# Four groups' softmax weights turned on TensorE instead of through DRAM, and one weight tile split earlier, in a fused attention and MLP kernel

## The chip, the cores and the metric

The kernel runs on one core of a Trainium2 chip. The metric is device time in microseconds (us) of one execution. Engines: PE is TensorE (matmuls; PEld loads its weights), DVE is VectorE, ACT is ScalarE, POOL is GpSimd, SP is SyncE, which here issues nearly all transfers. SPq and the like are an engine's sequencer.

## The reference

Three stages in float32, each feeding the next:

```python
# attention inside chunks of 64 rows; B=4, H=8, S=576, D=64
scores = scale * np.matmul(q_c, k_c.transpose(0, 1, 2, 4, 3))
scores = scores - np.max(scores, axis=-1, keepdims=True)
attn = np.exp(scores)
attn = attn / (np.sum(attn, axis=-1, keepdims=True) + 1e-09)
out = np.matmul(attn, v_c)
x = out.transpose(0, 2, 1, 3).reshape(B * S, H * D)        # 2304 x 512
# first MLP: 512 -> 2048 -> 512
h = x @ w_in
g = np.maximum(h, 0.0) + alpha * np.minimum(h, 0.0)
x = g @ w_out
# second MLP: 512 -> 1536 twice, their product, -> 512
a = x @ w_a
b = x @ w_b
return a * b @ w_out
```

## The kernel before

**Tiles.** Tokens are worked in five blocks of 512, 256, 512, 512 and 512 (b = 0 to 4), and attention in 18 groups u of 128 tokens, two chunks of each of the eight heads at a time. Every float32 operand of an MLP matmul is split into a rounded high part and the remainder (names ending in h and l; `to_hi` on ACT, `to_lo` on DVE), and each product is made of three matmuls, high by high, low by high, high by low. The last two blocks are worked as a pair, with sums and differences of blocks and of weights (names p, t, ys, wit; the banks psA, psB, psD, psE), so that seven products do the work of eight.

**Loops.** The first three blocks run through 16 slices j of the hidden dimension each: twelve matmuls into psh (line 392), the bend on ACT and DVE (neg, pos, gh, gl), twelve matmuls into acc. The attention of the pair, groups 10 to 17, is woven into the loop of block b = 2, from about 174 to 300 us, by `att_line` (line 1065): a table gives each step its slot, and slot 2j or 2j + 1 stands beside slice j. The order on every engine is the order in which the code emits; nothing reorders it.

**One group's way.** POOL loads k and q of a group (`load_kq`, line 245) into a staging tile. `apart` has ACT split each into two planes of 16-bit halves (kqd, line 262) and SP write these to rows in DRAM (rowsk, rowsq, line 264). `turn_qk` has SP read them back transposed (kT, qT; DMA_TRANSPOSE, line 269). `multiply` makes the scores (`att_S`, line 311, bank psSO) and in the same two banks, with the transposed weights of a group three places earlier, the output (`att_O`, line 368). `soften` takes the maximum, exp (line 332), the sum and the division; the result is e, the softmax weights. The output's matmuls need e transposed (eT). For groups from `P_DMA` = 10 on, `att_PT_out` splits e on ACT (ed, line 262) and has SP write rowse; `att_PT_in`, two slots later, has SP read it back transposed as eT. For groups 0 to 9, `att_PT` does the same on chip: four transposes on PE (line 350) into a bank psP, and one ACT copy (line 352). psP comes from a pool of four banks that psh and psSO use as well.

SP's queue is in order: an instruction that waits for rows to land holds all behind it.

**The pair's first MLP.** `group1(jp)` (line 1366 and on) works two slices of the pair's weights at once. While one group of products runs, the steps of the next group's weights (`t_steps`: the sums and differences wit, and the splits Txh and Txl, txh and txl) are collected in a list, and `rest()` emits them at the end of the group's other work.

Of the kernel before, what the change touches and what calls it, by code (L numbers as in the profile page):

```python
# [18 lines left out]
def chunk_attention_prelu_mlp_bilinear_mlp(  # L19
# [19 lines left out]
    B, H, S, D = q.shape  # L39
# [6 lines left out]
    KD = DM // P  # L46
# [42 lines left out]
    def to_lo(hi, lo, src):  # L89
        if lo is None:  # L90
            return
        nc.vector.tensor_tensor(out=lo, in0=src, in1=hi.bitcast(F32), op=ALU.subtract)  # L92
# [164 lines left out]
    P_DMA = 10  # L257
# [82 lines left out]
        yield nc.vector.reciprocal(out=rc, in_=sm)  # L340
        yield nc.vector.tensor_tensor(out=e3, in0=e3, in1=rc.to_broadcast([P, H, CH]), op=ALU.mult)

    def att_PT(u):
        e_ = att.pop(("e", u))
        if u >= P_DMA:
            att["eT", u] = turned(halves(e_, wtile(f"ed{u}", F32), f"e{u}"), f"eT{u}")
            return
        ps = att_bank(u, "psP")
        for g in range(KD):
            nc.tensor.transpose(ps[:, g * P:(g + 1) * P], e_[:, g * P:(g + 1) * P], ident)  # L350
        t = wtile(f"eT{u}", F32)
        nc.scalar.activation(out=t, in_=ps, func=AF.Copy)
        att["eT", u] = t
# [185 lines left out]
    def stagger(chains):  # L539
        steps = [c[0] for c in chains[:1]]  # L540
        for i, c in enumerate(chains):
            steps += [d[0] for d in chains[i + 1:i + 2]] + c[1:]
        return steps
# [521 lines left out]
    def att_line(bx, x, ut, sums_of):  # L1065

        t0, n = blocks[bx]
        us = range(t0 // P, NU)
        LAG = 3

        def dest(u):
            if u * P < t0 + n:
                return *x, u * P - t0
            ut[u] = wtile(f"x{u}", F32).rearrange("p (k t) -> p k t", k=KD)
            return ut[u], None, 0

        def out_of(u, pss):
            o = att_O(u, *dest(u), pss)
            if u + LAG < NU:
                load_v(u + LAG, nc.gpsimd)  # L1080
            return o

        def multiply(w):
            pss = [bank("psSO") for _ in range(2)]
            now, then_ = us[w:w + 1], us[max(w - LAG, 0):max(w - LAG + 1, 0)]
            for u in now:
                att_S(u, [ps[:, :KD * CH] for ps in pss])
            o = sum((out_of(u, [ps[:, KD * CH:] for ps in pss]) for u in then_), [])
            each(to_hi, o)

            def after():
                for u in now:
                    att_M(u)
                each(to_lo, o)

            return after

        def soften(u):
            att_X(u)
            return lambda: weave(att_N(u))  # L1100

        def out_only(*ws):
            pss = [bank("psSO") for _ in range(2)]
            o = sum((out_of(us[w], [ps[:, i * KD * CH:(i + 1) * KD * CH] for ps in pss])
                     for i, w in enumerate(ws)), [])
            each(to_hi, o)
            return lambda: each(to_lo, o)

        def only(fn, *a):
            def step():  # L1110
                fn(*a)
                return lambda: None

            return step

        at = {
            "S": (0, 3, 6, 10, 13, 16, 19, 22), "out": (3, 7, 9, 13, 17, 19, 21, 25),
            "apart": (None, None, 1, 5, 7, 11, 13, 17), "load": (None, None, None, 1, 4, 7, 10, 13),
        }
        steps = [(slot, lambda w=w: multiply(w)) for w, slot in enumerate(at["S"])]  # L1120
        steps += [(slot + 1, lambda u=u: soften(u)) for u, slot in zip(us, at["S"])]
        steps += [(slot + 2, only(att_PT_in, u)) for u, slot in zip(us, at["out"])]
        steps += [(slot + 2, only(turn_qk, u)) for u, slot in zip(us, at["apart"]) if slot]
        steps += [(slot, only(att_PT_out, u)) for u, slot in zip(us, at["out"])]
        steps += [(slot, only(apart, u)) for u, slot in zip(us, at["apart"]) if slot]
        steps += [(slot, only(load_kq, u, True, nc.gpsimd)) for u, slot in zip(us, at["load"]) if slot]
        steps += [(2, only(load_v, us[2], nc.gpsimd))]
        steps += [(slot, lambda w=w: out_only(w)) for w, slot in ((5, 24), (6, 27), (7, 29))]
        steps += [(slot, only(fn)) for slot, fn in sums_of]
        return sorted(steps, key=lambda s: s[0])  # L1130

    with tc.manual_schedule():
# [131 lines left out]
        for b, (t0, n) in enumerate(blocks[:bx]):  # L1264
            nxt = xtiles("x")
            if b + 1 < bx:
                steps = att_steps(b + 1, nxt)
            else:
# [5 lines left out]
                def begin_t():  # L1274
# [5 lines left out]
                steps = att_line(bx, nxt, ut, (  # L1280
                    (20, lambda: load_raw(0)), (24, begin_t),
                    (23, lambda: y_sums(0)), (26, lambda: y_sums(1)), (28, lambda: y_sums(2)), (31, lambda: y_sums(3)),
                ))
# [81 lines left out]
        def later(j, g):  # L1365
            def second():
                if acc[0] is None:
                    acc[0] = new_acc()
                s2(j, g[:2], acc[0], NB)

            pend.append(second)
# [8 lines left out]
        def group1(jp):  # L1380

            A, B, D, E = (bank(nm) for nm in ("psA", "psB", "psD", "psE"))

            def tt(out_, a, b_):
                nc.vector.tensor_tensor(out=out_, in0=a, in1=b_, op=ALU.add)  # L1385

            more = []
            if jp + 2 < J1 // 2:
                load_raw(jp + 2)
            if jp + 1 < J1 // 2:  # L1390
                more, four = t_steps(jp + 1)
                more += stagger(four)

            def staged(nm):
                both_ = sp.tile([P, 2, DM], F32, tag="stg", name=nm)
                return both_[:, 0], both_[:, 1]

            def copied(out_, src):
                nc.scalar.activation(out=out_, in_=src, func=AF.Copy)

            def first_x():
                neg = below(A)
                g = halves_of(tp.tile([P, NB], F32, tag="t", name="pos"))
                bent(2 * jp, neg, A, g[2])
                return g

            def rest():
                while more:
                    more.pop(0)[1]()

            product1(A, jp, "11", 0, True)
            if jp == 0:
                p1, t1 = staged("p1")
                copied(p1, A)
                product1(E, jp, "22", 7, True)
                product1(A, jp, "12", 1, False)
                g0 = first_x()
                product1(B, jp, "s2", 5, True)
                tt(t1, p1, B)
                to_hi(*g0)  # L1420
                product1(D, jp, "s1", 4, True)
                p5, t2 = staged("p5")
                copied(p5, D)
                to_lo(*g0)
                later(0, g0)
                product1(B, jp, "s3", 6, False)
                tt(t2, p1, B)
                product1(D, jp, "s4", 3, False)
                tt(t1, t1, D)
                n1_ = below(t1)  # L1430
                rest()
                bent(1, n1_, t1, t1)
                g1 = halves_of(t1)
                to_hi(*g1)
                tt(p5, t2, p5)
                to_lo(*g1)
                later(1, g1)
            else:
                tail.pop(0)()
                p1, t1 = staged("p1")  # L1440
                copied(p1, A)
                product1(B, jp, "s2", 5, True)
                tail.pop(0)()
                tt(t1, p1, B)
                flush(0)
                rest()
                for fn in asides.get(jp, ()):
                    fn()
                product1(D, jp, "s1", 4, True)
                p5, t2 = staged("p5")  # L1450
                copied(p5, D)
                product1(A, jp, "12", 1, False)
                g0 = first_x()
                product1(D, jp, "s4", 3, False)
                tt(t1, t1, D)
                to_hi(*g0)
                n1_ = below(t1)
                to_lo(*g0)
                later(2 * jp, g0)
                bent(2 * jp + 1, n1_, t1, t1)  # L1460
                product1(B, jp, "s3", 6, False)
                tt(t2, p1, B)
                g1 = halves_of(t1)
                to_hi(*g1)
                tt(p5, t2, p5)
                product1(E, jp, "22", 7, True)
                to_lo(*g1)
                later(2 * jp + 1, g1)
            tt(p1, t2, E)
            tail.extend([lambda: to_y(2 * jp + 1, p5), lambda: to_y(2 * jp, p1)])  # L1470
# [169 lines left out]
```

## Time and profile before

| what | us |
|---|---|
| median of three runs | 875.88 |
| the three runs | 875.88, 879.87, 874.39 |
| the profiled execution | 874.59 |
| its span, first to last instruction | 872.8 |
| PE busy | 842.4 (97%) |
| DVE busy | 658.7 (75%) |
| ACT busy | 409.8 (47%) |
| POOL busy | 25.4 (3%) |
| waits of PE for qT | 12.9 |

The profile is of one execution, and all times in it are counted from the span's start. A row of a timeline gives the start, the duration, the engine, the line, the operation, the tile written and those read, the shape and, in brackets, how long the engine stood idle before it and what ended that. Of several instructions of a kind in a row (x30) only one row is shown, with the time from the first start to the last end. Matmuls overlap, so a row's duration is longer than its slot: in a run of them the slot is the difference of two starts. The granted clock of TensorE is given as a share of its full speed. DMA is the mean busy share of the core's 16 DMA engines.

### The profile page before, as it was taken

The page shows a single profiled execution, that of the slowest core. Times are in us where ns is not written, and L with a number is a line of the kernel's source. Part 1 is how long each engine was busy: PE and PEld are TensorE (multiplying, and loading weights), DVE is VectorE, ACT ScalarE, POOL GpSimd, SP SyncE. Part 2 cuts the span into 40 slices and gives each one's busy share as a digit, 9 for nine tenths or more (in the row PEclk, how much of TensorE's full clock was granted, in tenths as well). Part 3 has the DMA queues.
Part 4 walks back from the last instruction along what each step waited for, and adds up shares of the span by engine and source line. Part 5 has one row for each costly group of instructions (what it writes and reads, how often), then busy time and mean ns, then how long its engine had stood idle before and what let it go on. Part 6 is the DMA issues. An engine that isn't in the chain of part 4 may idle for free.

```text
span 872.8 us, 14507 instructions
## 1 busy us (share of the span) xinstructions
PE 842.4 (97%) x5430; PEld 719.7 (82%) x5430; DVE 658.7 (75%) x1269; ACT 409.8 (47%) x777; POOL 25.4 (3%) x41
## 2 busy tenths in 40 slices
PE   6999999997799999999999999999999999999998
PEld 5778889975577778888888888888888888889998
DVE  5999975663558787685997898898898858848782
ACT  4677775553455644443753333332232226634440
POOL 0000000023100000000000000000000000000000
PEclk9999999998989999999999999999999999999999
DMA  9796769688893222123660264464464238935421
GB/s 215 176 250 209 208 158 235 169 200 181 153 227 103 105 73 97 49 66 139 235 212 24 85 241 139 139 223 138 139 223 139 91 100 305 304 100 182 129 78 50
DMA packets 151672, 137.29 MB, mean 157 GB/s; under 512 B 82225, under 2 KB 118577, under 8 KB 151601
## 3 DMA queue, kind: packets, MB, share of 16 engines
q1 hardware_dynamic: 148992, 127.97, 49.6%
q0 software_dynamic: 2608, 8.39, 4.0%
q8 instruction: 43, 0.70, 0.4%
q14 instruction: 29, 0.23, 0.1%
HBM read 82.32 MB, written 45.61 MB: 147 GB/s over the span
## 4 chain that ended last, share of the span: by engine, by line
PE 79%; DVE 8%; DMA 5%; ACT 4%; issue 2%; SPq 1%; DVEq 0%; ACTq 0%
PE acc L392 21%; PE psh L392 7%; PE psA L610 7%; PE psB L610 7%; PE psD L610 7%; PE psE L610 4%; PE psr L392 3%; PE psD L754 3%; PE psB L754 3%; PE psA L754 3%; PE psA L1342 3%; PE psB L1342 3%; PE psD L1342 2%; DMA qT<-rowsq 2%; PE psE L754 1%
## 5 line engine op out<-in xcount | busy, mean ns | idle before, releaser
L412 DVE SCALAR_TENSOR_TENSOR pos<-neg,nalpha_sb,pos 128x512 f32<-128x512 f32 (+1 forms) x48 | 31.6, 658 | 44.8 <-ACT pos L411 44.7
L148 DVE SCALAR_TENSOR_TENSOR wx<-wx,wz 128x512 int32<-128x512 int32 x68 | 46.8, 688 | 13.5 <-ACT wx L136 11.6
L92 DVE TENSOR_TENSOR gl<-pos,gh 128x512 fp32r<-128x512 f32 (+1 forms) x56 | 34.4, 615 | 21.8 <-ACT gh L87 21.1
L87 ACT ACTIVATE gh<-pos 128x512 fp32r<-128x512 f32 (+1 forms) x56 | 32.0, 571 | 39.0 <-DVE pos L412 32.5
L640 DVE TENSOR_TENSOR t<-p,psB 128x512 f32<-128x512 f32 x48 | 32.9, 685 | 21.1 <-PE psB L610 16.9
L644 ACT ACTIVATE p<-psA 128x512 f32<-128x512 f32 x24 | 14.4, 598 | 71.7 <-PE psA L610 71.7
L136 ACT ACTIVATE wx<-raw 128x512 f32<-128x512 f32 x68 | 42.8, 670 | 1.4 <-DMA raw<-in_moe_w_out_dram 1.4
L650 ACT ACTIVATE p<-psD 128x512 f32<-128x512 f32 x24 | 14.4, 599 | 50.9 <-PE psD L610 42.4
L140 DVE TENSOR_SCALAR wz<-raw 128x512 uint16<-128x512 uint16 x68 | 31.2, 459 | 0.5 <-DMA raw<-in_moe_w_out_dram 0.5
L145 DVE TENSOR_SCALAR wz<-raw 128x512 uint16<-128x512 uint16 x68 | 30.8, 453 | 0.0
L678 ACT ACTIVATE b_sb<-psr 128x256 f32<-128x256 f32 x12 | 4.6, 382 | 51.2 <-PE psr L392 51.2
L1356 DVE SCALAR_TENSOR_TENSOR pos<-neg,beta_sb,psA 128x512 f32<-128x512 f32 x8 | 6.0, 748 | 28.6 <-ACT neg L1352 28.6
L410 ACT ACTIVATE neg<-psh 128x512 f32<-128x512 f32 (+1 forms) x48 | 24.8, 516 | 5.2 <-PE psh L392 5.2
L392 PE MATMUL psr<-xrh,Tl 128*128 128x256 f32 x96 | 27.2, 283 | 0.0
L392 PE MATMUL psr<-xrl,Th 128*128 128x256 f32 x96 | 27.2, 283 | 0.0
L392 PE MATMUL psr<-xrh,Th 128*128 128x256 f32 x96 | 27.1, 282 | 0.0
L411 ACT ACTIVATE pos<-psh 128x512 f32<-128x512 f32 (+1 forms) x48 | 25.1, 524 | 0.0
L262 ACT ACTIVATE kqd<-kq 128x1024 uint16<-128x1024 uint16 x24 | 24.1, 1049 | 1.7 <-DMA kq<-in_k_dram 1.3
L311 PE MATMUL psSO<-kT,qT 64*64 64x64 f32 x448 | 10.9, 237 | 14.1 <-DMA qT<-rowsq 12.9
L311 PEld LDWEIGHTS psSO<-kT,qT 64*64 64x64 f32 x448 | 9.2, 146 | 17.8 <-issue 16.4
L1352 ACT ACTIVATE neg<-p 128x512 f32<-128x512 f32 x24 | 15.2, 632 | 9.7 <-DVE p L1385 8.9
L332 ACT ACTIVATE e<-e 128x512 f32<-128x512 f32 x18 | 11.3, 629 | 16.3 <-DVE e L326 16.3
(948 smaller groups left out, 3017.0 us busy)
## 6 DMA issues: line engine op xcount, KB each, us to landing
raw<-in_moe_w_out_dram SPq DMA_DIRECT2D x28, 512.0 KB, 3.6
raw<-in_moe_w_in_dram SPq DMA_DIRECT2D x16, 512.0 KB, 5.3
raw<-in_moe_w_a_dram SPq DMA_DIRECT2D x12, 512.0 KB, 4.9
raw<-in_moe_w_b_dram SPq DMA_DIRECT2D x12, 512.0 KB, 4.9
cd<-t SPq DMA_DIRECT2D x24, 256.0 KB, 2.2
cd<-p SPq DMA_DIRECT2D x24, 256.0 KB, 2.0
wd<-wi POOLq DMA_DIRECT2D x16, 256.0 KB, 3.8
wir<-wd SPq DMA_DIRECT2D x16, 256.0 KB, 3.0
```

The costliest lines, as they stand in the source:

```text
L87: nc.scalar.activation(out=hi, in_=src, func=AF.Copy)
L92: nc.vector.tensor_tensor(out=lo, in0=src, in1=hi.bitcast(F32), op=ALU.subtract)
L136: return nc.scalar.activation(out=x.bitcast(F32), in_=hw.bitcast(F32), func=AF.Copy, scale=2.0 ** -112)
L140: yield nc.vector.tensor_scalar(out=z2[:, :, 0], in0=h2[:, :, 1], scalar1=13, scalar2=None, op0=ALU.logical_shift_right)
L145: yield nc.vector.tensor_scalar(out=z2[:, :, 1], in0=h2[:, :, 3], scalar1=1 << 15, scalar2=None, op0=ALU.bitwise_and)
L148: yield nc.vector.scalar_tensor_tensor(out=x, in0=x, scalar=3, in1=z, op0=ALU.logical_shift_left, op1=ALU.bitwise_or)
L392: nc.tensor.matmul(out=ps, lhsT=a, rhs=b, start=(i == 0 and first), stop=(i == n_i - 1 and a is wl))
L412: yield nc.vector.scalar_tensor_tensor(out=pos, in0=neg, scalar=nalpha_sb[:, j:j + 1], in1=pos, op0=ALU.mult, op1=ALU.add)
L610: nc.tensor.matmul(out=ps, lhsT=a, rhs=b, start=(start and kk == 0 and i == 0), stop=(kk == 1 and i == 2), skip_group_check=not start,)
L640: nc.vector.tensor_tensor(out=out, in0=a, in1=b, op=op)
L754: nc.tensor.matmul(out=ps[:, s * HALF:(s + 1) * HALF], lhsT=a, rhs=x[:, e], start=(start and s == 0 and i == 0 and n == 0), stop=(i == J2 ...
L1342: nc.tensor.matmul(out=ps, lhsT=a, rhs=b_, start=(start and kk == 0 and i == 0), stop=(kk == 1 and i == 2), skip_group_check=not start,)
```

## The change

It has two parts.

The first: the softmax weights of groups 10 to 13 take the way on chip that groups 0 to 9 take. `att_PT` gets a flag for it, and the table an entry "turn" with their slots, 5, 8, 11 and 14. Groups 14 to 17 keep the way through DRAM, at the slots they had.

The second: in the first pass of `group1`, the first step list of the second group's weights, the split of its first tile (Txh and Txl), is taken out of what `rest()` emits and is emitted right behind `to_lo(*g0)`.

```diff
@@ -340,9 +340,9 @@
         yield nc.vector.reciprocal(out=rc, in_=sm)
         yield nc.vector.tensor_tensor(out=e3, in0=e3, in1=rc.to_broadcast([P, H, CH]), op=ALU.mult)
 
-    def att_PT(u):
+    def att_PT(u, by_pe=False):
         e_ = att.pop(("e", u))
-        if u >= P_DMA:
+        if u >= P_DMA and not by_pe:
             att["eT", u] = turned(halves(e_, wtile(f"ed{u}", F32), f"e{u}"), f"eT{u}")
             return
         ps = att_bank(u, "psP")
@@ -1114,14 +1114,15 @@
             return step
 
         at = {
-            "S": (0, 3, 6, 10, 13, 16, 19, 22), "out": (3, 7, 9, 13, 17, 19, 21, 25),
+            "S": (0, 3, 6, 10, 13, 16, 19, 22), "turn": (5, 8, 11, 14), "out": (17, 19, 21, 25),
             "apart": (None, None, 1, 5, 7, 11, 13, 17), "load": (None, None, None, 1, 4, 7, 10, 13),
         }
         steps = [(slot, lambda w=w: multiply(w)) for w, slot in enumerate(at["S"])]
         steps += [(slot + 1, lambda u=u: soften(u)) for u, slot in zip(us, at["S"])]
-        steps += [(slot + 2, only(att_PT_in, u)) for u, slot in zip(us, at["out"])]
+        steps += [(slot, only(att_PT, u, True)) for u, slot in zip(us, at["turn"])]
+        steps += [(slot + 2, only(att_PT_in, u)) for u, slot in zip(us[KD:], at["out"])]
         steps += [(slot + 2, only(turn_qk, u)) for u, slot in zip(us, at["apart"]) if slot]
-        steps += [(slot, only(att_PT_out, u)) for u, slot in zip(us, at["out"])]
+        steps += [(slot, only(att_PT_out, u)) for u, slot in zip(us[KD:], at["out"])]
         steps += [(slot, only(apart, u)) for u, slot in zip(us, at["apart"]) if slot]
         steps += [(slot, only(load_kq, u, True, nc.gpsimd)) for u, slot in zip(us, at["load"]) if slot]
         steps += [(2, only(load_v, us[2], nc.gpsimd))]
@@ -1389,6 +1390,8 @@
                 load_raw(jp + 2)
             if jp + 1 < J1 // 2:
                 more, four = t_steps(jp + 1)
+                if jp == 0:
+                    soon = four.pop(0)
                 more += stagger(four)
 
             def staged(nm):
@@ -1422,6 +1425,8 @@
                 p5, t2 = staged("p5")
                 copied(p5, D)
                 to_lo(*g0)
+                for _, fn in soon:
+                    fn()
                 later(0, g0)
                 product1(B, jp, "s3", 6, False)
                 tt(t2, p1, B)
```

**SP, from group 12's transposes to group 14's rows.** The rows as the program has them before; qT_2715 is group 12's, rowse_2719 holds group 10's weights, and the next rowsk, rowsq, kT and qT are group 13's.

```order
L269 DMA_TRANSPOSE qT_2715<-rowsq_2635 128x4x256
L264 DMA rowse_2719<-ed_2717 128x1024
L269 DMA_TRANSPOSE eT_2776<-rowse_2719 128x4x256
L264 DMA rowsk_2780<-kqd 128x1024
L264 DMA rowsq_2783<-kqd 128x1024
L269 DMA_TRANSPOSE kT_2848<-rowsk_2780 128x4x256
L269 DMA_TRANSPOSE qT_2850<-rowsq_2783 128x4x256
L264 DMA rowse_2854<-ed_2852 128x1024
L264 DMA rowsk_2858<-kqd 128x1024
L264 DMA rowsq_2861<-kqd 128x1024
L269 DMA_TRANSPOSE eT_2906<-rowse_2854 128x4x256
```

The same stretch now:

```order
L269 DMA_TRANSPOSE qT_2715<-rowsq_2635 128x4x256
L264 DMA rowsk_2781<-kqd 128x1024
L264 DMA rowsq_2784<-kqd 128x1024
L269 DMA_TRANSPOSE kT_2849<-rowsk_2781 128x4x256
L269 DMA_TRANSPOSE qT_2851<-rowsq_2784 128x4x256
L264 DMA rowsk_2855<-kqd 128x1024
L264 DMA rowsq_2858<-kqd 128x1024
```

The writes of rowse and the transposes eT are gone, four of each in the whole stretch; nothing else on SP changes places.

**PE, at the first turn.** The piece of the difference between slices 0 and 3 of block 2's loop; the other three turns stand in front of acc wo2, psh wi6 and acc wo5.

```order
 L392 MATMUL acc<-gl,wo0h 128x512
 L392 MATMUL acc<-gh,wo0l 128x512
+L350 MATMUL psP<-ident,e_2610 128x128 x4
 L392 MATMUL psh<-xh,wi3h 128x512
 L392 MATMUL psh<-xl,wi3h 128x512
```

Four transposes are put between two runs of twelve matmuls, at each of the four places.

**ACT, around the first two turns.** How the program with the change has it; kqd of kq_2637 is group 13's, that of kq_2738 group 14's, and eT_2777 and eT_2887 are groups 10 and 11.

```order
L352 ACTIVATE eT_2777<-psP 128x512
L262 ACTIVATE kqd<-kq_2637 128x1024 x2
L410 ACTIVATE neg<-psh 128x512
L411 ACTIVATE pos<-psh 128x512
L87 ACTIVATE gh<-pos 128x512
L332 ACTIVATE e_2829<-e_2829 128x512
L262 ACTIVATE kqd<-kq_2738 128x1024 x2
L352 ACTIVATE eT_2887<-psP 128x512
L410 ACTIVATE neg<-psh 128x512
```

The copies eT take the place of the four splits ed of these groups: the first and the third stand ahead of the splits of group 13 and of group 15, the second behind those of group 14, and the fourth behind the exp of group 14.

**DVE, at the pair's second group of weights.** Before, behind the bend of the first slice (pos):

```order
L1356 SCALAR_TENSOR_TENSOR pos<-neg,beta_sb,psA 128x512
L1385 TENSOR_TENSOR p_3940<-p_3940,psB 128x512
L92 TENSOR_TENSOR gl<-pos,gh 128x512
L1385 TENSOR_TENSOR p_3974<-p_3940,psB 128x512
L1385 TENSOR_TENSOR p_3940<-p_3940,psD 128x512
L1214 TENSOR_TENSOR wit<-wir 128x256
L1214 TENSOR_TENSOR wit<-wir,wit 128x256
L1214 TENSOR_TENSOR wit<-wir 128x256
L1214 TENSOR_TENSOR wit<-wir,wit 128x256
L92 TENSOR_TENSOR Txl<-wir,Txh 128x512
L92 TENSOR_TENSOR txl<-wit,txh 128x512
```

Now:

```order
L1357 SCALAR_TENSOR_TENSOR pos<-neg,beta_sb,psA 128x512
L1386 TENSOR_TENSOR p_3944<-p_3944,psB 128x512
L92 TENSOR_TENSOR gl<-pos,gh 128x512
L92 TENSOR_TENSOR Txl<-wir,Txh 128x512
L1386 TENSOR_TENSOR p_3978<-p_3944,psB 128x512
L1386 TENSOR_TENSOR p_3944<-p_3944,psD 128x512
L1215 TENSOR_TENSOR wit<-wir 128x256
```

Txl stands six places earlier on DVE, and on ACT Txh stands one place earlier, ahead of neg.

## Rows read from the trace of the kernel before

**Rows 1.** Waits of PE, whole span: total us, times, longest.

```profile
PE psSO L311 <- DMA qT<-rowsq: 12.9, 3, 6.4
...
PE psP L350 <- ACT eT L352: 1.7, 1, 1.7
```

**Rows 2.** The chain that ended last, two stretches: start us, us, what.

```profile
156.56 0.44 PE psP L350 x4
...
204.11 9.21 DMA qT<-rowsq
...
215.64 3.68 PE acc L392 x12
...
221.32 3.50 DMA qT<-rowsq
...
231.74 8.98 DMA qT<-rowsq
...
252.09 0.62 PE psSO L311 x32
...
253.19 2.95 PE psh L392 x12
```

**Rows 3.** Timeline of PE around the three waits.

```profile
206.63 0.39 PE L392 MATMUL psh<-xh,wi5l 128*128 128x512 f32 x1
213.45 1.23 PE L311 MATMUL psSO<-kT,qT 64*64 64x64 f32 x30 [6.44 <-DMA qT<-rowsq]
...
224.96 0.76 PE L311 MATMUL psSO<-kT,qT 64*64 64x64 f32 x30 [0.19 <-DMA qT<-rowsq]
...
240.86 1.14 PE L311 MATMUL psSO<-kT,qT 64*64 64x64 f32 x30 [6.22 <-DMA qT<-rowsq]
```

**Rows 4.** Windows: us, busy of PE, PEld, DVE, ACT, POOL; clock, DMA, GB/s.

```profile
213.00:217.00 4.00, 3.55 (x67) 3.19 (x68) 0.00 (x0) 1.50 (x4) 0.00 (x0) 0.50 1.07 331
241.00:245.00 4.00, 4.00 (x70) 3.51 (x71) 0.46 (x1) 1.64 (x4) 0.00 (x0) 0.56 1.04 261
```

**Rows 5.** Waits of SP between 190 and 262 us.

```profile
SPq L269 <- DMA rowse<-ed: 22.8, 5, 7.5
```

**Rows 6.** Timeline of SP: issue of transfers.

```profile
197.33 1.28 SPq L269 DMA_TRANSPOSE eT<-rowse  x1
198.66 0.64 SPq L264 DMA_DIRECT2D rowsk<-kqd  x1
...
228.03 0.56 SPq L264 DMA_DIRECT2D rowsk<-kqd  x1
```

**Rows 7.** Timeline of ACT: the splits into planes.

```profile
193.48 1.99 ACT L262 ACTIVATE kqd<-kq 128x1024 uint16<-128x1024 uint16 x2
...
200.62 1.04 ACT L262 ACTIVATE ed<-e 128x1024 uint16<-128x1024 uint16 x1
...
221.21 1.99 ACT L262 ACTIVATE kqd<-kq 128x1024 uint16<-128x1024 uint16 x2
```

**Rows 8.** Timeline of POOL: the load of k of group 17.

```profile
231.60 0.88 POOL L245 DMA_DIRECT2D kq<-in_k_dram  x1 [19.41 <-ACT pos L411]
```

**Rows 9.** Line 352 grouped: ns min/median/max, first and last start us.

```profile
L352 ACT ACTIVATE eT<-psP x10: 578/598/634, 15.3 to 168.8; 128x512 f32<-128x512 f32 x10
```

**Rows 10.** Timelines of PE, ACT and DVE at the pair's second group.

```profile
306.67 0.39 PE L1342 MATMUL psD<-ys4h,Txl 128*128 128x512 f32 x1
309.01 0.51 PE L1342 MATMUL psA<-xh,Txh 128*128 128x512 f32 x1 [1.96 <-ACT Txh L87]
...
313.64 0.40 PE L392 MATMUL acc<-gh,wo0h 128*128 128x512 f32 x1
...
307.81 0.63 ACT L1352 ACTIVATE neg<-p 128x512 f32<-128x512 f32 x1 [2.79 <-DVE p L1385]
...
305.73 0.69 DVE L1385 TENSOR_TENSOR p<-p,psB 128x512 f32<-128x512 f32 x1 [1.31 <-PE psB L1342]
...
308.15 0.42 DVE L1214 TENSOR_TENSOR wit<-wir,wit 128x256 f32<-128x256 f32 x1
```

## The prediction

> **What bounds the kernel now.** I read the page first: PE is busy 842.4 of 872.8 us (97%), so a change pays only where PE waits. The waits of PE [rows 1] name one that is long: the scores matmul (line 311) waits three times for a transposed q, 12.9 us in all. The timeline of PE [rows 3] places these in the loop of the third block: 6.44 us before group 13's scores, 0.19 before group 14's, 6.22 before group 15's (groups are numbered 0 to 17; S13, qT13 and so on belong to group 13): 12.85 us.
>
> Each long wait costs more than itself. In the stretch after it the granted clock is 0.50, after S15 0.56 [rows 4], which is the lower of TensorE's two levels, 1.2 GHz for 2.4; before, PE had lain idle for over 6 us. From S13's start at 213.45 to the end of the twelve matmuls behind it (215.64 + 3.68 = 219.32) are 5.87 us; the same work from S16, which had no wait, is 252.09 to 253.19 + 2.95 = 256.14, so 4.05 [rows 2]. The difference, 1.82 us, is the clock's price at S13.
>
> Next I asked why qT is late. Its chain is in-order work on SP: rows of k and q to DRAM, then kT, then qT. SP's waits [rows 5] show that it stood 22.8 us, five times, for the rows of softmax weights (rowse) to land, so that it could issue their transposes (eT). In SP's timeline [rows 6] eT10 goes out at 197.33 and rowsk13 only behind it, at 198.66, although ACT had begun both splits of group 13 at 193.48, 1.99 us for the two [rows 7], so k's was done at about 194.5. For group 15 the same: splits from 221.21, so k's done at about 222.2, rowsk15 at 228.03. It is the head of SP's queue that blocks, and the change takes just these heads away.
>
> **Part 1: the softmax weights of groups 10 to 13.** Removed: four rowse writes and four eT transposes from SP, four splits of 1.04 us on ACT [rows 7]. Added: four times four transposes on PE, at 0.44 us a group in the chain of waits [rows 2], and four ACT copies of 0.60 [rows 9]. ACT's work shrinks by 4 x (1.04 - 0.60) = 1.8 us, which I count as nothing: ACT is busy 47% and what hides it is PE's own work; without that cover 4 x 0.60 would be the most it costs. POOL's queue stands as before, and its loads of k and q still wait for rows to land, which now happens earlier.
>
> PE's new work lies on the path: 4 x 0.44 = 1.8 us.
>
> *S13.* PE was ready at 206.63 + 0.39 = 207.0; two of the transposes are ahead of it, so 207.9. The rows of group 13 now wait only for their split, which has the copy of eT10 ahead: 193.48 + 0.60 + 1.0 = 195.1. From rowsk's issue to qT's landing took 198.66 to 204.11 + 9.21 = 213.32, so 14.66 us for group 13 and 228.03 to 231.74 + 8.98 = 240.72, so 12.69 us for group 15 [rows 2, 6]. That gives 207.8 to 209.8, a wait of 0 to 1.9 us. I take 1.0, the middle: S13 at 208.9 instead of 213.45.
>
> *S14.* PE was ready at 224.96 - 0.19 = 224.77, 11.32 us after S13. Less 1.8 for the clock and with one transpose, 9.9 us: 218.8. qT14 landed 11.50 us after qT13 (221.32 + 3.50 = 224.82); this held an issue of eT11 and its wait for rowse11. From 207.8 with nothing of these left to 209.8 + 11.50 = 221.3, the wait is 0 to 2.5. I take 0.4, near the bottom, since what SP waited for is gone.
>
> *S15.* PE was ready at 240.86 - 6.22 = 234.64, which is 9.68 us behind S14; with one transpose, 10.1 from 219.2: 229.3. The splits began 7.76 us after S13. With 0.60 for eT12's copy ahead of them, and with or without the 1.8 of the clock, they come 6.5 to 8.4 us after 208.9; k's is done at 216.4 to 218.3, by the middle at 217.3. Adding group 15's own 12.69 gives 230.0, adding 14.66 gives 232.0; the extremes are 229.1 and 233.0, a wait of 0 to 3.7. I take 1.2, between 0.7 (its own row) and 1.7 (the middle).
>
> *The clock.* 1.8 us at S13 by the rows; I take the same at S15, whose stretch has almost the same granted clock: 3.6 us. The bound below is that S15 gives nothing back, 1.8.
>
> Sum of part 1: 12.85 - (1.0 + 0.4 + 1.2) + 3.6 - 1.8 = 12.05 us gained.
>
> **Part 2: the first weight tile of the second group.** PE ends psD at 306.67 + 0.39 = 307.06 and then waits 1.96 us for Txh, which ACT makes only at the end of a queue that was idle: it stood 2.79 us, from 305.02 to 307.81, for a DVE sum [rows 10]. The change puts Txh into that hole, 305.0 to 305.6, and Txl behind it on DVE, 305.6 to 306.3, where DVE had 1.31 us of idle time before a sum that started at 305.73. That sum is moved by at most 0.56 us. psA can then start at 307.07, 1.9 us earlier. What is late next is psB's weight tile, whose differences DVE makes at 308.15 and later; txh follows at about 308.57 + 0.61 = 309.2 and its lower half 0.69 behind its last difference, at about 309.9. With this wait I put the start of the output matmuls at 310.8. They stand at 313.64 now, 4.63 us behind psA's start for twelve matmuls, which take 2.95 elsewhere [rows 2]. So the gain is 313.64 - 310.8 = 2.8 us. The bounds are 313.64 - (307.07 + 2.95) = 3.6, if nothing waits, and 0, if psB's wait takes the place of psA's and the lower clock stays.
>
> **The sum** is made against the profiled execution, 874.59 us (872.8 and 1.8 around the span): 874.59 - 12.05 - 2.8 = 859.7. PE's next longest waits in the list are of 2.0 us (that for Txh) and of 1.7 [rows 1], so no queue behind these places is there to take the gain back. The median of the three runs is 875.88, 1.29 above the profiled one, so in its terms the answer is 859.7 to 861.0; I say 860.0.
>
> **Rivals.**
>
> *S15 keeps its wait, S13 loses its own.* qT15 is issued at 231.74, and POOL's load of k for group 17 starts at 231.60 [rows 2, 8]; that load waits for group 15's rows and so moves with qT15. If the transposes then take as long as in the worst row, the wait grows from 1.2 back to 6.2 and the clock stays down: 859.7 + 5.0 + 1.8 = 866.5. Against: rowsk15 goes out some 10 us earlier in any case. Chance 0.12.
>
> *The transfers, not the queue.* qT15, beside POOL's load of k, took 8.98 us and qT13 9.21; qT14, issued at 221.32, 3.50 [rows 2, 8]. DMA's mean busy share is 1.07 and 1.04 in the stretches of rows 4. If it is the amount of data that sets the landing, an earlier issue only stretches it, all 12.85 us and the clock stay, and 1.8 of transposes is added: 874.59 + 1.8 - 2.8 = 873.6. Against: eight transfers of the loop are gone, and the 22.8 us in which SP stood for rowse [rows 5] are no transfer of q or k. Chance 0.08. The Trainium skill, page "DMA: Bandwidth & Descriptors", section "Issuing engines are not separate DMA queues", speaks for this rival: transfers from any engine run on the same 16 DMA engines and interleave, and issuing from several saves only the sequencer's time, usually small. By that rule POOL's loads and SP's transposes stretch each other, and the 9.21 against 3.50 agrees; the 22.8 us of SP's waits do not, since by it an issuing queue costs little.
>
> *Slower: banks held by the copies.* The transposes take a bank of the pool that psh and psSO also use, and give it back with ACT's copy. At two of the four places a copy stands behind or beside the splits of k and q (1.99 us). If each copy came after splits, neg and pos (0.52 each by the page) and itself, 1.99 + 1.04 + 0.60 = 3.6 us, and PE wanted the bank at once, that would be 4 x 3.6 = 14.5 us of waits, with the clock lost each time (4 x 1.8): 859.7 + 21.7 = 881.4, slower than now. It decides from the point where a copy ends later than the next twelve matmuls do, 2.95 us. For it: earlier in the program PE waited once, 1.7 us, for such a copy [rows 1]. Against: two of the copies have no split ahead of them, and the pool has four banks. Chance 0.03.
>
> **Numbers.** Forecast 0.77, rivals 0.12, 0.08 and 0.03. The range: below, no waits left (-2.6) and part 2 in full (-0.8), 856; above, the waits at their upper bounds (+0.9, +2.1, +2.5), S15's clock not given back (+1.8) and part 2 at nothing (+2.8) make 869.8, not likely all together: 869, which holds the first rival too. About 1% (8.8 us) is what a measurement of this kernel can tell from no change. The forecast lies 1.8% below; the first rival, 866.5, just at the bound. So faster 0.84, same 0.14, slower 0.02.
>
> **What would show it.** On SP no rowse and no eT before group 14's, and rowsk13 at about 195; S13 at 208 to 210 with under 2 us of wait, S15 at 229 to 232, the granted clock near 1.00 behind both; qT waits of PE under 5 us in sum instead of 12.9. At the second group psA without a wait for Txh and the output matmuls some 2.8 us sooner behind psD. Wrong would be: rowsk13 early but qT13 as late as now; a wait of PE for the copy of eT; a new wait of psB as long as psA's was.

## The result and the profile after

The kernel with the change took 862.63 us (median of four runs, 860.99 to 865.36) against 875.13 for the kernel before in the same comparison (873.95 to 879.87): 0.985 of the time, 95% interval 0.9803 to 0.9897. A second measurement gave 860.7 us (six runs, 857.95 to 861.93) against 874.74: 0.984, interval 0.981 to 0.9869. Forecast were 860.0 and a range of 856 to 869. The first profiled execution took 863.86 us, 10.7 less than before's 874.59; the one of the second measurement 858.4. Both are used here, since they differ in the one place that matters most.

The page's head and PE's waits (total us, times, longest) of the first:

```profile
span 862.1 us, 14526 instructions
...
PE 840.3 (97%) x5446; PEld 718.7 (83%) x5446; DVE 658.7 (76%) x1269; ACT 409.0 (47%) x777; POOL 25.4 (3%) x41
...
PE psSO L311 <- DMA qT<-rowsq: 6.1, 2, 5.3
```

The waits for qT fell from 12.9 us [rows 1] to 6.1. PE's timeline shows where they are:

```profile
206.64 0.69 PE L311 MATMUL psSO<-kT,qT 64*64 64x64 f32 x32
...
216.64 0.88 PE L311 MATMUL psSO<-kT,qT 64*64 64x64 f32 x30
...
232.24 1.13 PE L311 MATMUL psSO<-kT,qT 64*64 64x64 f32 x32 [5.32 <-DMA qT<-rowsq]
```

S13 and S14 have no wait left, where rows 3 have 6.44 and 0.19. S15 still waits 5.32 of its 6.22. (The other 0.76 us of the 6.1 is at S12; in before's execution PE stood 1.27 us there.)

SP's timeline answers to rows 6:

```profile
194.40 0.35 SPq L264 DMA_DIRECT2D rowsk<-kqd  x1
...
199.81 1.25 SPq L269 DMA_TRANSPOSE qT<-rowsq  x1
...
215.10 0.34 SPq L264 DMA_DIRECT2D rowsk<-kqd  x1
...
220.98 1.25 SPq L269 DMA_TRANSPOSE kT<-rowsk  x1
222.34 1.23 SPq L269 DMA_TRANSPOSE qT<-rowsq  x1
```

rowsk13 goes out at 194.40 instead of 198.66, rowsk15 at 215.10 instead of 228.03. SP's long waits (190 to 262 us) are now for rows of k:

```profile
SPq L269 <- DMA rowsk<-kqd: 19.5, 4, 9.2
SPq L264 <- ACT kqd L262: 11.3, 8, 5.9
SPq L269 <- DMA rowse<-ed: 6.0, 2, 4.6
```

The 22.8 us for rowse [rows 5] are 6.0, all from groups 14 on. What SP now waits for is the group's own chain.

At S15 the chain of waits and the windows (us, busy of PE, PEld, DVE, ACT, POOL, granted clock, DMA share, GB/s) read:

```profile
222.34 9.76 DMA qT<-rowsq
...
232.24 1.13 PE psSO L311 x32
233.38 0.85 PE psSO L368 x32
234.23 3.92 PE acc L392 x12
```

```profile
228.00:232.00 4.00, 0.00 (x0) 0.00 (x0) 0.00 (x0) 0.00 (x0) 0.00 (x0) 0.68 0.70 178
232.00:236.00 4.00, 3.76 (x68) 3.32 (x69) 0.08 (x1) 1.64 (x4) 0.00 (x0) 0.50 0.60 190
```

So qT15 took 9.76 us to land (8.98 in rows 2), PE stood idle, and the clock behind it is at the lower level again, as in rows 4.

The second profiled execution of the same program, the same place:

```profile
219.55 7.61 DMA qT<-rowsq
...
227.30 0.69 PE psSO L311 x32
```

```profile
PE psSO L311 <- DMA qT<-rowsq: 0.6, 1, 0.6
```

```profile
232.00:236.00 4.00, 4.00 (x20) 3.30 (x18) 3.86 (x11) 2.34 (x3) 0.00 (x0) 1.00 0.34 59
```

Here S15 waits 0.6 us and the clock stays at its full level. From S15 to S16 pass 227.30 to 236.77 = 9.47 us, against 232.24 to 243.52 = 11.28 in the first: 1.81 us, the lower clock's price. With the longer wait, 4.72, that is 6.5 us, more than the 5.46 by which the two executions differ. So this one place is enough to make the difference.

The pair's second group of the first execution, on PE, then ACT and DVE:

```profile
298.45 0.39 PE L1343 MATMUL psD<-ys4h,Txl 128*128 128x512 f32 x1
298.69 0.40 PE L1343 MATMUL psA<-xh,Txh 128*128 128x512 f32 x1
...
301.10 0.50 PE L1343 MATMUL psB<-ys2h,txh 128*128 128x512 f32 x1 [0.87 <-ACT txh L87]
...
302.85 0.39 PE L392 MATMUL acc<-gh,wo0h 128*128 128x512 f32 x1
```

```profile
296.54 0.60 ACT L1402 ACTIVATE p<-psD 128x512 f32<-128x512 f32 x1 [1.33 <-DMA x2d<-xs]
297.04 0.62 ACT L87 ACTIVATE Txh<-wir 128x512 fp32r<-128x512 f32 x1
...
297.69 0.69 DVE L92 TENSOR_TENSOR Txl<-wir,Txh 128x512 fp32r<-128x512 f32 x1 [1.76 <-ACT Txh L87]
```

psA follows psD without a wait, psB waits 0.87 us for txh. From psD's last matmul to the output's first are 302.85 - 298.45 = 4.40 us, against 313.64 - 306.67 = 6.97 [rows 10]: 2.57 us gained.

### The profile page after: what moved, and what is told of

The parts are those of the page before. It is cut to its first block, busy times and chain, and to the rows that moved or that the text cites. A ratio compares the mean times of both kernels' runs of the same rounds, so it can differ in the third digit from the quotient of the medians.

```text
span 862.1 us, 14526 instructions
## 1 busy us (share of the span) xinstructions
PE 840.3 (97%) x5446; PEld 718.7 (83%) x5446; DVE 658.7 (76%) x1269; ACT 409.0 (47%) x777; POOL 25.4 (3%) x41
## 4 chain that ended last, share of the span: by engine, by line
PE 84%; DVE 7%; DMA 4%; ACT 3%; issue 1%; SPq 0%; DVEq 0%; ACTq 0%
PE acc L392 24%; PE psh L392 9%; PE psA L610 8%; PE psD L610 8%; PE psB L610 8%; PE psr L392 4%; PE psE L610 4%; PE psD L754 3%; PE psB L754 3%; PE psA L754 3%; PE psB L1343 2%; PE psA L1343 2%; PE psD L1343 2%; DMA qT<-rowsq 2%; PE psE L754 2%; PE psSO L311 1%
## 5 line engine op out<-in xcount | busy, mean ns | idle before, releaser
L392 PEld LDWEIGHTS psr<-xrl,Th 128*128 128x128 f32 x96 | 18.4, 192 | 0.4
L392 PEld LDWEIGHTS psr<-xrh,Th 128*128 128x128 f32 x96 | 18.4, 192 | 0.4
```

The costliest lines, as they stand in the source:

```text
L392: nc.tensor.matmul(out=ps, lhsT=a, rhs=b, start=(i == 0 and first), stop=(i == n_i - 1 and a is wl))
```

## The experiments

**Each part alone.** `part1_only` takes the two places of `soon` out of the change, `part2_only` puts only them into the kernel before.

```diff
@@ -1391,6 +1391,4 @@
-                if jp == 0:
-                    soon = four.pop(0)
@@ -1426,6 +1424,4 @@
-                for _, fn in soon:
-                    fn()
```

> Only the four groups' softmax weights are turned on PE; the weight tile is split where it was. Theory: part 1 carries three quarters of the gain, 7.9 us of the 10.7 that the two profiled executions differ by: about 0.991 of before; qT waits of PE near 6 us, all at group 15, and psA of the second group waits 2.0 us for Txh again. Rival (the two parts only gain together, or part 2 gains nothing because psB's wait takes its place): the time of the whole change, 0.985.

> Only the weight tile is split earlier; the softmax weights go through DRAM as before. Theory: the output matmuls of the pair's first group start 2.3 to 2.8 us sooner behind psD's last matmul, about 0.997 of before; psB waits about 0.9 us for txh in place of psA's 2.0 for Txh. Rival: the new wait and a later sum on DVE eat it, 1.000.

Measured: part 1 alone 865.9 us, 0.9902 (0.9866 to 0.9939); part 2 alone 871.92 us, 0.9973 (0.9953 to 0.9993), both against 874.13. By the ratios that is 8.6 and 2.4 us. Their sum, 11.0, and the 12.5 of 875.13 that both give together agree within the intervals; nothing here shows that one part needs the other. Part 1's qT waits in its profiled execution were not all at group 15, as expected, but 3.58 us at S15, 0.74 at S14 and 2.39 at S12 (listed there under DVE; see `late15` below). With part 2 alone, PE at the second group reads:

```profile
303.27 0.39 PE L1342 MATMUL psD<-ys4h,Txl 128*128 128x512 f32 x1
...
307.66 0.39 PE L392 MATMUL acc<-gh,wo0h 128*128 128x512 f32 x1
```

That is 4.39 us where it was 6.97 before, so part 2 works without part 1. PE at the second group with part 1 alone, and the window behind the wait:

```profile
299.07 0.39 PE L1343 MATMUL psD<-ys4h,Txl 128*128 128x512 f32 x1
301.42 0.50 PE L1343 MATMUL psA<-xh,Txh 128*128 128x512 f32 x1 [1.97 <-ACT Txh L87]
...
304.72 0.39 PE L392 MATMUL acc<-gh,wo0h 128*128 128x512 f32 x1
```

```profile
301.00:303.00 2.00, 1.42 (x5) 0.90 (x6) 2.00 (x5) 1.72 (x4) 0.00 (x0) 1.00 0.00 0
```

The wait for Txh is there as before, but the clock does not fall behind it: 304.72 - 299.07 = 5.65 us instead of 6.97. So 1.3 of part 2's 2.57 us is the lower clock, which in before's profiled execution followed this wait and in this one did not (nor in `queue_only`, below, where the same wait was 1.96 us and the distance 5.64); the sure gain is 5.65 - 4.40 = 1.25 us. The timed 2.4 lies between.

**The queue without the traffic.** `queue_only` is the kernel before with eT's transposes behind the rows in their slot.

```diff
-        steps += [(slot + 2, only(att_PT_in, u)) for u, slot in zip(us, at["out"])]
         steps += [(slot + 2, only(turn_qk, u)) for u, slot in zip(us, at["apart"]) if slot]
         steps += [(slot, only(att_PT_out, u)) for u, slot in zip(us, at["out"])]
         steps += [(slot, only(apart, u)) for u, slot in zip(us, at["apart"]) if slot]
+        steps += [(slot + 2, only(att_PT_in, u)) for u, slot in zip(us, at["out"])]
```

> The kernel before with one thing changed: eT's transposes of all eight groups are issued behind the rows of k and q that share their slot, instead of ahead of them. No transfer is removed and PE gets no transposes. Theory (SP's queue head was what made qT late): rowsk13 goes out at about 195 instead of 198.7, and the wait at S13 falls from 6.4 us to between 0 and 3; with the clock behind it that is 4 to 8 us, 0.991 to 0.995 of before. Rival (the amount of data on the 16 DMA engines sets qT's landing): rowsk13 goes out early, qT13 lands as late as before, the waits stay near 12.9 us and the time is that of before, 1.000.

Measured: 870.24 us against 874.13, 0.9954 (0.9935 to 0.9974). SP, PE and the chain:

```profile
194.30 0.35 SPq L264 DMA_DIRECT2D rowsk<-kqd  x1
```

```profile
210.83 0.75 PE L311 MATMUL psSO<-kT,qT 64*64 64x64 f32 x30 [2.85 <-DMA qT<-rowsq]
...
224.74 0.69 PE L368 MATMUL psSO<-eT,v 64*64 64x64 f32 x32 [2.05 <-DMA eT<-rowse]
...
237.20 0.75 PE L311 MATMUL psSO<-kT,qT 64*64 64x64 f32 x30 [1.79 <-DMA qT<-rowsq]
```

```profile
199.66 11.03 DMA qT<-rowsq
...
226.51 10.56 DMA qT<-rowsq
```

No transfer is removed and PE turns nothing more, yet S13's wait falls from 6.44 to 2.85 and S15's from 6.22 to 1.79: SP's queue was part of the cause. But qT13 and qT15 now take 11.03 and 10.56 us to land, where they took 9.21 and 8.98: an earlier issue is partly paid back in a longer transfer. And the new order makes waits of its own: PE stands 2.05 us at 224.74 and 0.35 later on for eT, for which it never waited in this loop before. The waits came out as the theory had them, and the time just short of its 4 to 8 us: the order alone, with these new waits taken off, is 3.9 of part 1's 8.6 us. That the removed traffic makes up the rest is the likely reading, not shown: part 1 also takes four splits from ACT. The sizes point that way without settling it: qT13 took 8.3 to 11.0 us in the three executions with rowse in the queue, and 4.9 to 9.4 in the eleven without.

**The loads beside qT15.** `no_kq17` takes POOL's two loads away that start with qT15; the kernel then leaves out group 17's inputs.

```diff
         att["kq", u] = a = pair(f"kq{u}", staged)
+        if u == NU - 1:
+            for t in a:
+                nc.gpsimd.memset(t, 0.0)
+            return
```

> The whole change, but POOL writes zeros into group 17's k and q instead of loading them, so two transfers of 256 KB that start beside qT15 are gone (group 17's attention is then computed from zeros). Theory (qT15 takes 9.8 us because these loads share the DMA engines with it): qT15 lands 4 us or less after its issue, S15's wait falls from 5.3 us to under 1 and its matmuls run at the full clock: 5 to 7 us below the whole change. Rival (group 15's rows are simply too late, or other transfers take the place of the loads): qT15 still takes 8 us or more and the wait stays at 4 to 5.5.

> As no_kq17 (zeros in place of group 17's k and q), timed. Theory (the loads beside qT15 make and spread its landing): qT15 lands within 4 us again, S15 does not wait, and the runs lie 2 to 6 us below the whole change. Rival (the first look fell on a lucky execution): qT15 takes 7 us or more, or S15 waits over 2.

Measured: 861.12 us in one execution, 2.7 below the profiled 863.86 and not the expected 5 to 7; timed 858.42 us (858.1 to 861.24), 0.9822 (0.979 to 0.9853). The transfer view of the stretch at qT15's issue (us to landing), first and second profiled execution:

```profile
qT<-rowsq SPq DMA_TRANSPOSE x1, 3.4
```

```profile
qT<-rowsq SPq DMA_TRANSPOSE x1, 4.4
```

3.4 and 4.4 us, against 9.76 and 7.61 with the loads, and S15 waits for nothing in either: in the first it starts at 231.02, right behind the matmuls ahead of it. So the loads stretch qT15; that is shown. The gain in time is less clear: the median is 2.3 to 4.2 us below the whole change's two, with the intervals overlapping. Both executions lost time ahead of S15, the second with waits of 2.1 us at S12 and 1.6 at S14, the first at S12 (the edit adds four lines, so line 311 is L315 there):

```profile
197.11 0.69 PE L315 MATMUL psSO<-kT,qT 64*64 64x64 f32 x32 [2.09 <-DMA qT<-rowsq]
```

The granted clock from 197 to 201 us was 0.64 there, and S15 came 4 us later than PE was ready for it in the change's first execution.

**The same program again.** 

> The whole change once more, for a second profiled execution. In all_turned, whose instructions are the same as the whole change's up to S15, qT15 took 7.1 us and S15 waited 0.6 us, against 9.8 and 5.3. Theory (how long POOL's loads and qT15 take side by side differs from execution to execution, so S15's wait is no fixed term): the wait at S15 comes out anywhere from 0 to 6 us, with the profiled time moving along, and the runs spread over 4 us or more; 0.985 of before. Rival (the wait is fixed by the program): S15 waits 4.8 to 5.8 us again.

The wait at S15 came out at 0.60 us (above) and the time at 860.7: the theory holds. Where the two executions part is seen behind rowsk15's issue, which is at the same time in both (215.10 and 215.14). The transfer view from there to kT15's issue, first execution (queue, packets, MB, share; then the transfer):

```profile
q0 software_dynamic: 216, 0.68, 58.2%
...
rowsk<-kqd SPq DMA_DIRECT2D x1, 256.0 KB, 5.8
```

and second:

```profile
q0 software_dynamic: 19, 0.03, 4.4%
...
rowsk<-kqd SPq DMA_DIRECT2D x1, 256.0 KB, 3.0
```

In the first, 0.68 MB of POOL's loads (queue q0) were still moving beside the rows, which took 5.8 us; in the second they were through, and the rows took 3.0. The 2.8 us between them, and the 2.15 by which qT15's own transfer differs (9.76 and 7.61), make the 4.9 us by which qT15 landed later, 4.7 of which are the longer wait. Group 16's loads had been issued at nearly the same time (208.84 and 208.95), yet from 200 to 215 us queue q0 had moved 1.16 MB in the first execution and 1.80 in the second. What lets POOL's loads end sooner in one execution than in another stays open.

**All eight groups on PE.** `all_turned` gives groups 14 to 17 the way on chip as well (the two lists of steps for the way through DRAM are then empty).

```diff
-            "S": (0, 3, 6, 10, 13, 16, 19, 22), "turn": (5, 8, 11, 14), "out": (17, 19, 21, 25),
+            "S": (0, 3, 6, 10, 13, 16, 19, 22), "turn": (5, 8, 11, 14, 17, 20, 23, 26), "out": (),
```

> The whole change, with groups 14 to 17 turned on PE too (slots 17, 20, 23, 26); no softmax weights go through DRAM in this loop. Theory: PE has no wait left there that SP's queue makes, so it only pays the transposes, 4 x 0.44 = 1.8 us, against at most the 1.3 us of PE's wait near 276: 0 to 2 us above the whole change, 0.985 to 0.987. Rival (fewer transfers speed up what is left): 2 us or more below it.

> Groups 14 to 17 turned on PE too, beside the whole change on the same chip. Theory (turning the last four on PE only pays transposes, and the 4 us it was ahead came from S15's wait as it happened to fall): within 0.3% of the whole change run beside it. Rival (with no softmax weights in DRAM at all, later stages gain too): 3 to 5 us below it, and the intervals apart.

Measured: 858.25 us, 0.9819 (0.9796 to 0.9841), and the second time 863.19 us (858.73 to 870.62), 0.9871 (0.983 to 0.9912). S15 in the two profiled executions:

```profile
226.58 0.69 PE L311 MATMUL psSO<-kT,qT 64*64 64x64 f32 x32 [0.57 <-DMA qT<-rowsq]
```

```profile
232.36 0.73 PE L311 MATMUL psSO<-kT,qT 64*64 64x64 f32 x32 [4.33 <-DMA qT<-rowsq]
```

The first time missed its expectation of 0 to 2 us above the whole change: 858.25 is 4.4 and 2.5 below the two medians, as its rival had it, and alone it would have made this a better kernel. The second time does not bear that out. Up to S15 its instructions are those of the change, and S15's wait again takes both values. The rival of 3 to 5 us less fell, and the theory's bound of 0.3% is just kept (863.19 beside 860.7).

**Group 15's rows earlier.** `early15` moves group 15's split one slot, and `all_turned_early15` does it beside all eight groups turned.

```diff
-            "apart": (None, None, 1, 5, 7, 11, 13, 17), "load": (None, None, None, 1, 4, 7, 10, 13),
+            "apart": (None, None, 1, 5, 7, 10, 13, 17), "load": (None, None, None, 1, 4, 7, 10, 13),
```

> The whole change, and group 15's split and rows one slot earlier (slot 10 instead of 11). Theory (S15 waits because its chain of rows, transposes and POOL's loads needs longer than the five slots it has): rowsk15 goes out at 210 to 212 instead of 215, S15's wait falls from 5.3 us to 1 to 3, 3 to 6 us below the whole change, about 0.980 of before. Rival (the DMA engines are full there, so an earlier issue only stretches the transfers): qT15 lands as late as now or takes qT14 with it, so that S14 waits instead; the time of the whole change, 0.985.

> All eight groups turned on PE, and group 15's rows one slot earlier. Theory (rows earlier take the wait off S15 and give part of it to S14, as in early15): 1 to 4 us below the whole change, about 0.981 of before. Rival: S14's wait comes in full for S15's, no gain over the whole change.

Measured: 859.19 us, 0.9833 (0.98 to 0.9866), and 858.85 us, 0.9822 (0.9794 to 0.9849). S14 in the one and in the other:

```profile
222.19 1.14 PE L311 MATMUL psSO<-kT,qT 64*64 64x64 f32 x30 [3.38 <-DMA qT<-rowsq]
```

```profile
218.81 0.75 PE L311 MATMUL psSO<-kT,qT 64*64 64x64 f32 x30 [1.62 <-DMA qT<-rowsq]
```

S15 waits in neither; S14 does, since group 15's rows now move beside qT14, which took 12.08 us to land in the first and 10.4 in the second. The wait went one group ahead, with 1.6 to 3.4 us of the 5.3. So theory and rival are each half right: S15's wait is gone, and S14 has one. The medians lie 1.5 to 3.8 us below the whole change's two, with the intervals overlapping, and are no lower than the first 858.25 of `all_turned`.

**S15 later.** `late15` moves S15 two slots, S16 and S17 one; `late15_turned` also turns all groups on PE.

```diff
@@ -1115,5 +1115,5 @@
-            "S": (0, 3, 6, 10, 13, 16, 19, 22), "turn": (5, 8, 11, 14), "out": (17, 19, 21, 25),
+            "S": (0, 3, 6, 10, 13, 18, 20, 23), "turn": (5, 8, 11, 14), "out": (17, 21, 23, 26),
@@ -1127,5 +1127,5 @@
-        steps += [(slot, lambda w=w: out_only(w)) for w, slot in ((5, 24), (6, 27), (7, 29))]
+        steps += [(slot, lambda w=w: out_only(w)) for w, slot in ((5, 25), (6, 28), (7, 30))]
```

> The whole change, with S15 two slots later (18 for 16), S16 and S17 one (20, 23), and what follows of groups 15 to 17 one or two slots later too. Theory: two slots are about 5.4 us of matmuls, as long as S15's wait, so PE works through it and the clock stays up: S15's wait 0 to 1 us, 5 to 7 us below the whole change, about 0.978 of before. Rival (the wait turns up behind: eT of the last groups, or the pair's first tiles, come too late at the loop's end): a new wait of 3 to 6 us of psSO for eT or of the second stage for ys, the time of the whole change or above.

> As late15, and groups 14 to 17 turned on PE too, so that no eT comes through DRAM at the loop's end. Theory: S15's wait is gone as in late15 and no eT can be late; 4 x 0.44 us of transposes more: 4 to 6 us below the whole change, 0.979. Rival: the end of the loop is bound by the sums for the second stage, which come one slot later: the gain of late15 is lost again, 0.985.

Measured: 861.65 us, 0.9849 (0.9823 to 0.9876), and 861.94 us, 0.9876 (0.9823 to 0.9929). Neither execution waits at S15; each lost time in another place, `late15` before S12 and `late15_turned` at the loop's end. The waits of PE of the one, and PE's timeline of the other:

```profile
PE psSO L311 <- DVE wi L159: 2.5, 1, 2.5
```

```profile
267.94 0.80 PE L392 MATMUL psh<-xh,wi14h 128*128 128x512 f32 x1 [3.31 <-ACT pos L411]
```

The second is the rival that was named: ACT stood behind the sums for the second stage. The first is put down to DVE, but S12 started at 197.01, and qT12, issued at 191.52, took 5.4 us, so it landed at 196.9: it is a wait for qT again. qT12 took 5.3 us in `part1_only` too (a wait of 2.4), and 3.6 in the change, whose instructions up to there are the same. It varies from one execution to the next, as S15's does. The expected 5 to 7 us did not show: the edit removes one wait of this kind, and in the profiled execution another came. What the other executions waited for is not shown.

## Why the prediction was right, and where its working was not

**What bounds the kernel.** Right: what moved are PE's waits and the clock behind them; its busy time, 842.4 before, is 840.3 us.

**S13 and S14.** Right in kind and a little cautious. Waits of 1.0 and 0.4 were taken; both are 0 in the two executions of the change. rowsk13 came at 194.4 (195.1 forecast), and qT13 landed 6.2 us behind its issue, not 9.2. The rows gave one transfer time for qT13, and it is no fixed one: the eleven executions that turn group 10 on PE have 4.9 to 9.4 us. S14, at 0 here, waits 0.36 to 1.55 us in three other executions whose instructions up to there are the same.

**S15.** This step failed in the first execution: 1.2 us were taken, at most 3.7 allowed, 5.32 measured. The splits were on time (rowsk15 at 215.10, k's split forecast to be done at 216.4 to 218.3); the 17.0 us from there to qT15's landing at 232.10 were above both rows used, 12.69 and 14.66; in the second execution they were 12.02, below both. The first rival named the mechanism, POOL's load that the landing of the same rows sets off, and `no_kq17` shows it. Its chance of 0.12 was too small, because the forecast read a wait that varies as one number: in the five executions whose instructions up to S15 are the change's it was 0.57, 0.60, 3.58, 4.33 and 5.32 us. A row of one execution gives such a wait's place, but not its size in the next. (The rival's 6.2 was the wait of the kernel before; its own worst row bounds the wait at 3.7.)

**The clock.** 1.82 us at S13: from its start to the end of the twelve matmuls behind are now 206.64 to 210.75 (207.80 + 2.95), 4.11 instead of 5.87, so 1.76. At S15 nothing came back in the first execution (232.24 to 238.15, 5.91 us), the bound that the range held; in the second all of it.

**The transposes.** Right: 0.44 us a group in the chain of waits of the change. The slow rival did not show: the only wait of PE for such a copy in this loop, in all runs, is one of 0.20 us in `late15_turned`.

```profile
200.81 0.44 PE psP L350 x4
```

**Part 2.** 2.8 us forecast, 2.57 measured in profile, 2.4 timed. psB's wait for txh was named and is 0.87 us. Not foreseen: the copy p waits 1.33 us for a staging tile that x2d's write still holds, so Txh comes only at 297.04, and the products into psD of ys4 start 0.15 us late. And the step took the lower clock behind psA's wait for a fixed part of the price.

**The sum.** Against the first execution the forecast of 859.7 was 4.2 short of 863.86: S15's wait +4.1, its clock +1.8, S13 and S14 -1.4, part 2 +0.2; that is +4.7. Outside these terms S10, which lies ahead of all that was changed, starts 0.65 us earlier (177.39, against 178.04), S12 waits 0.5 less, and at 276.48 PE waits 1.34 us for y22h, where 0.37 stood before; with these it is 4.5, and 0.3 is not traced. Against the second, 858.4, the forecast was 1.3 above. That it lies only 2.6 and 0.7 us from the two medians is in part luck: S13 and S14 were put 1.4 too high, and S15's wait, put at 1.2, came out anywhere between 0.6 and 5.3.

**The second rival,** that the transfers and not the queue set the landing, was half right: `queue_only` moved the rows 4.4 us forward and got 3.6 us of wait at S13, with the transfer 1.8 us longer. The Trainium skill's page "DMA: Bandwidth & Descriptors", section "Issuing engines are not separate DMA queues", says that transfers issued by different engines run on the same 16 DMA engines and interleave. The trace agrees at S15: 3.4 and 4.4 us without POOL's loads, 9.76 and 7.61 with them. What the section counts for the issuing queue is the sequencer's time to start a transfer, usually small; of an instruction that waits at the head of a queue it does not speak. Here that was the costly part: SP's in-order queue stood 22.8 us for rowse, and the order alone was worth 3.9 us.

## What to carry to other kernels

A wait for a transfer is read in two parts: when it was issued, and how long it took beside what else was moving. The order of the queue that issues it is in the program and can be changed for good; the time in flight, and with it the issue of what waits for that landing, changed here with the traffic and from one execution to the next, so it belongs in the range, not in the sum. Before a late transfer is counted as repaired, look for what its own chain sets off at the same moment: here the rows whose landing let qT15 go also let two loads go.

## What was not expected of the hardware

- One program, two executions: qT15's transfer took 9.76 and 7.61 us, the rows ahead of it 5.8 and 3.0, and PE's wait 5.32 and 0.60.
- qT12's transfer took 3.4 to 3.7 us in eight executions and 4.9 to 5.4 in five, and S12 waits up to 2.5 us for it. POOL's loads for group 14 started 0.55 to 0.63 us behind its issue in the eight, and 0.46 to 0.52 behind it in the five. Whether that start decides it, no run shows.
- The clock falls behind some short waits and not behind others. In 4 us at the restart behind waits of 3.38 us (S14 of `early15`), 3.58 (S15 of `part1_only`) and 4.33 (S15 of `all_turned`, second time) the granted clock was 0.57, 0.57 and 0.61. Behind S12's wait of 2.45 us in `late15` it was 0.57, behind 2.09 in `no_kq17` 0.64, behind 2.39 in `part1_only` and 2.48 in `queue_only` 1.00; in 2 us behind psA's 1.96 us 0.50 in the kernel before, behind its 1.97 with part 1 alone 1.00. The windows behind S12, `late15` and then `part1_only`:

```profile
197.00:201.00 4.00, 3.99 (x40) 3.31 (x41) 2.77 (x6) 1.10 (x3) 1.94 (x3) 0.57 0.83 246
196.60:200.60 4.00, 3.97 (x46) 3.32 (x47) 2.77 (x6) 1.09 (x3) 1.89 (x3) 1.00 0.82 250
```
